# Moving w2 and the two halves of h by 128 bytes in the expert stage's on-chip memory layout

## The chip, the cores and the metric

The kernel runs on one core of a Trainium2 chip. The metric is the device time of one execution in microseconds (us). TensorE (PE in the rows) does the matrix products, VectorE (DVE) and ScalarE (ACT) the elementwise work, GpSimd (POOL) issues scattered transfers, SyncE (SP) the other ones.

## The reference

```
X = rfft(x, axis=1)                       # x: 8 x 2496 x 256
Yr = Xr @ w_r - Xi @ w_i + b_r            # and Yi likewise; soft threshold 0.01 on both
t = irfft(Yr + i*Yi).reshape(19968, 256)  # the tokens
expert = argmax(t @ w_gate); g = its softmax weight
out[token] = g * (relu(token @ w1[expert]) @ w2[expert])   # 8 experts, 256 -> 1024 -> 256
```

All inputs are float32. The first four lines are the spectral stage, the last one is the expert stage.

## The kernel before, in words

The spectral stage transforms batch after batch and scatters each token's row into a list of its expert in DRAM. The expert stage then works through tiles of 256 tokens of one expert each; 82 tiles run. Every float32 operand of a product is split into a high part, rounded to the format in which TensorE takes one column per step, and a low part, the rest. Products are sums of three partial products.

A tile of the expert stage gives TensorE three streams, always in this order:

- the **up stream**, line 1097: 48 matmuls of 256 columns. The moving operand is the tile's input, `xh` or `xl`; the stationary operand, loaded by a weight load (LDWEIGHTS) before each matmul, is 128 columns of w1, `h1` or `l1`. The order is (h1, xh), (l1, xh), (h1, xl), for two halves of the depth and eight groups of 128 hidden units.
- the **wide stream**, line 1137: 16 matmuls of 512 columns. Moving is `h2`, in which w2's high and low part lie side by side; stationary is the high half of h, `hh`.
- the **low stream**, line 1139: 16 matmuls of 256 columns. Moving is the high part of w2 in `h2`; stationary is the low half of h, `hl`.

ScalarE makes `hh` from the up stream's sums (line 1102), VectorE makes `hl` (line 1103). From the eighth tile on the wide and low streams run for both halves of the tile's tokens together: 16 wide matmuls in a row, then 16 low ones. The tiles before it, whose work is interleaved with the end of the spectral stage, and the last tile go through `down`'s loop over `h`: 8 wide, 8 low, and the same again.

All of these tiles lie in the pool `w2p`. The function `skip` allocates a small unused tile, so that what comes after it starts at a chosen byte offset. The sums of the allocations give these offsets, modulo 256 bytes:

| tile | used as | before | after |
|---|---|---|---|
| `h1`, `l1` (pool `k2`) | stationary, up | 0 | 0 |
| `xh`, `xl` | moving, up | 192 | 192 |
| `h2` (w2) | moving, wide and low | 64 | 192 |
| `hh` | stationary, wide | 64 | 192 |
| `hl` | stationary, low | 128 | 0 |
| `xf`, the transposed input | not read by TensorE | 64 | 192 |
| `o`, `part` | not read by TensorE | 128 | 0 |

Every slice that a matmul or a weight load takes of these tiles starts a multiple of 512 bytes behind the tile, so the offset of a tile is that of all its slices. In the spectral stage line 413 multiplies with moving w at offset 192 and stationary `sh` or `sl` at 0, and line 345 has both operands at 192.

Of the kernel before, what the change touches and what calls it, by code (L numbers as in the profile page):

```python
# [99 lines left out]
class Kernel:  # L100
# [849 lines left out]
    def open_experts(self, st):  # L950
        self.w2p = self.pool(st, "w2p", 1, side="right")
        self.psa = self.pool(st, "psa", 2, side="right", space=PSUM)
        self.psb = None
        self.wide = False
        self.r2 = [self.w2p.tile([128, 4, D], F32, name=f"r2{q}") for q in range(2)]
        self.weights(0, 2)
        self.skip(self.w2p, 64)
        self.h2 = self.w2p.tile([128, 8, 2, D], F32R, name="h2")

    def word(self, j, t, top):  # L960
# [94 lines left out]
    def upright(self, t):  # L1055
        if t >= self.nt:
            return
        nc = self.nc
        xf = self.w2p.tile([128, 2, 8, 32], F32, tag="xf", name="xf")
        nc.vector.transpose(xf.rearrange("p c t j -> p t c j"), self.xqs.pop(t))  # L1060
        yield
        xf = xf.rearrange("p c t j -> p c (t j)")
        if not t:
            self.skip(self.w2p, 128)
        xh = self.w2p.tile([128, 2, TT], F32R, tag="xh2", name="xh2", bufs=2)
        xl = self.w2p.tile([128, 2, TT], F32R, tag="xl2", name="xl2", bufs=2)
        with self.tc.high_priority():
            nc.scalar.copy(xh, xf)
        yield
        with self.tc.high_priority():  # L1070
            nc.vector.tensor_sub(xl, xf, xh)
        self.xts[t] = (xh, xl)

    def up(self, t, work=()):
        work = iter(work)
        nc = self.nc
        xh, xl = self.xts.pop(t)
        h1, l1 = self.h1, self.l1
        if t and self.psb:
            self.split2(t)  # L1080
        if not t:
            self.skip(self.w2p, 192)
        hh = self.w2p.tile([128, 8, TT], F32R, tag="hh", name="hh")
        if not t:
            self.skip(self.w2p, 64)
        hl = self.w2p.tile([128, 8, TT], F32R, tag="hl", name="hl")
        for f2 in range(4):
            if f2 % 2 and self.wide:
                p = self.psi.tile([128, 512], F32, tag="u", name="ph", bufs=4).rearrange("p (i t) -> p i t", i=2)
            else:  # L1090
                p = (self.psb if self.psb and f2 % 2 else self.psa).tile([128, 2, TT], F32, tag="h", name="ph")
            for i in range(2):
                f = f2 * 2 + i
                m = 0
                for c in range(2):
                    for a, v in ((h1, xh), (l1, xh), (h1, xl)):
                        nc.tensor.matmul(p[:, i, :], a[:, c, f * 128:(f + 1) * 128], v[:, c, :],  # L1097
                                         start=m == 0, stop=m == 5)
                        m += 1
            s = slice(f2 * 2, f2 * 2 + 2)  # L1100
            with self.tc.high_priority():
                nc.scalar.activation(hh[:, s, :], p, AF.Relu)  # L1102
                nc.vector.scalar_tensor_tensor(out=hl[:, s, :], in0=p, scalar=0.0, in1=hh[:, s, :],  # L1103
                                               op0=ALU.max, op1=ALU.subtract)
            next(work, None)
            if t and f2 % 2 == 0 and not self.psb:
                self.split2(t, (f2, f2 + 1))
            if t > 1 and f2 % 2:
                self.pace(hh.bitcast(F32)[0:1, f2 * 2, 0:1])
                self.send(1)  # L1110
            yield
        self.hs[t] = (hh, hl)

    def down(self, t):
        tc, nc = self.tc, self.nc
        hh, hl = self.hs.pop(t)
        w2 = self.h2
        xr = self.xrs.pop(t)
        if t >= self.early:
            row = self.w2p.tile([128, 2], I32, tag="row", name="row", bufs=2)  # L1120
            nc.vector.tensor_tensor(out=row, in0=xr.bitcast(I32)[:, :, 1], in1=self.drop[:, t - self.early, :],
                                    op=ALU.add)
            at = [row[:, h:h + 1] for h in range(2)]
        else:
            at = [xr.bitcast(I32)[:, h, 1:2] for h in range(2)]
        o = self.w2p.tile([128, 2, D], F32, tag="o", name="o", bufs=2)
        if t == self.early:
            self.skip(self.w2p, 32)

        def bank():  # L1130
            return (self.psb.tile([128, 512], F32, tag="o", name="po") if self.psb else
                    self.psi.tile([128, 512], F32, tag="u", name="po", bufs=4))

        def product(p, h, f, wide):
            hs = slice(h * 128, (h + 1) * 128)
            if wide:
                nc.tensor.matmul(p, hh[:, f, hs], w2[:, f].rearrange("p a d -> p (a d)"), start=f == 0, stop=False)  # L1137
            else:
                nc.tensor.matmul(p[:, :D], hl[:, f, hs], w2[:, f, 0, :], start=False, stop=f == 7)  # L1139

        def give(p, h):
            part = self.w2p.tile([128, D], F32, tag="part", name="part", bufs=2)
            nc.scalar.activation(part, p[:, D:], AF.Copy, scale=xr[:, h, 0:1])  # L1143
            nc.vector.scalar_tensor_tensor(out=o[:, h, :], in0=p[:, :D], scalar=xr[:, h, 0:1], in1=part,  # L1144
                                           op0=ALU.mult, op1=ALU.add)
            i = nc.gpsimd.indirect_dma_start(  # L1146
                out=self.out[:, :], out_offset=bass.IndirectOffsetOnAxis(ap=at[h], axis=0),
                in_=o[:, h, :], in_offset=None, bounds_check=self.ntok - 1, oob_is_err=False)
            if t or h:
                tc.declare_no_dep(i.ins, group="out", reason="every token is in one tile only")  # L1150
            tc.add_to_no_dep_group("out", i.ins)

        if self.psb and t < self.final:
            ps = [bank() for _ in range(2)]
            for wide in (True, False):
                for f in range(8):
                    for h in range(2):
                        product(ps[h], h, f, wide)
                if wide:
                    self.split1(t + 1)  # L1160
                    yield
            for h in range(2):
                give(ps[h], h)
            yield
            return
        for h in range(2):
            p = bank()
            for wide in (True, False):
                for f in range(8):
                    product(p, h, f, wide)  # L1170
                if wide and t < 2:
                    yield
            if not h:
                self.split1(t + 1)
            give(p, h)
            yield
# [56 lines left out]
```

## Time and profile before

| | us |
|---|---|
| median of 3 runs (1460.29 to 1462.82) | 1460.95 |
| the profiled execution | 1460.41 |
| its span, first to last instruction | 1458.6 |
| TensorE busy in it | 1436.8 |
| VectorE, ScalarE, GpSimd busy | 926.7, 767.5, 477.9 |

Matmuls are pipelined: a matmul's duration in a row (277 ns for one of line 1097) reaches into the next one. What a stream costs is read from the starts of its matmuls: the time from the first start of one stream to the first start of the next, divided by the count.

### The profile page before, as it was taken

How to read it: one execution, taken by the hardware profiler on the slowest of the kernel's cores; microseconds unless marked ns; L12 is line 12 of the kernel's file. 1: busy time of each engine (PE TensorE's matmuls, PEld its weight loads, DVE VectorE, ACT ScalarE, POOL GpSimd, SP SyncE). 2: the span in 40 equal slices, each digit the busy share in tenths (PEclk: the TensorE clock that was granted, in tenths of full speed). 3: DMA queues.
4: the chain of work that ended last, by engine and by line, in shares of the span. 5: the costliest groups of instructions: out<-in, count | busy, mean ns of one | idle time of the engine just before them, and what ended most of it. 6: DMA issues, size and time to landing. Idle time of an engine off the chain costs nothing. (4 is left out here: it accounts for less than half of the span.)

```text
span 1458.6 us, 34965 instructions
## 1 busy us (share of the span) xinstructions
PE 1436.8 (99%) x10551; PEld 1310.5 (90%) x10552; DVE 926.7 (64%) x1951; ACT 767.5 (53%) x1537; POOL 477.9 (33%) x594
## 2 busy tenths in 40 slices
PE   8999999999999999999999999999999999999997
PEld 4889898898989878899999999999999999999996
DVE  3788898988998876554565645454545445445443
ACT  2778787787877764444443434343434334334332
POOL 3042466656574354343311211211211121111111
PEclk9999999999999999999999999999999999999999
DMA  7974465556555333344332423233223223232210
GB/s 230 251 229 129 138 188 161 162 168 174 159 157 152 73 100 100 96 126 126 96 107 74 111 50 100 77 81 98 58 49 97 50 55 99 51 82 68 50 48 21
DMA packets 194337, 161.99 MB, mean 111 GB/s; under 512 B 128011, under 2 KB 164531, under 8 KB 194128
## 3 DMA queue, kind: packets, MB, share of 16 engines
q1 hardware_dynamic: 173616, 113.37, 30.7%
q0 software_dynamic: 20512, 46.20, 9.3%
q8 instruction: 87, 1.43, 0.4%
q14 instruction: 122, 1.00, 0.2%
HBM read 241.99 MB, written 66.37 MB: 211 GB/s over the span
## 5 line engine op out<-in xcount | busy, mean ns | idle before, releaser
L1097 PE MATMUL ph<-xh,h 128*128 128x256 f32 x1312 | 363.6, 277 | 0.0
L1097 PE MATMUL ph<-xl,h 128*128 128x256 f32 x1312 | 363.2, 277 | 0.0
L1097 PE MATMUL ph<-xh,l 128*128 128x256 f32 x1312 | 363.1, 277 | 0.0
L1137 PE MATMUL po<-h,hh 128*128 128x512 f32 x1312 | 313.5, 390 | 0.4 <-DVE h L1036 0.4
L1146 POOL DMA_INDIRECT out<-o,row x124 | 121.7, 981 | 558.0 <-DVE o L1144 527.4
L1103 DVE SCALAR_TENSOR_TENSOR hl<-ph,hh 128x512 fp32r<-128x512 f32 x328 | 225.9, 689 | 110.5 <-ACT hh L1102 95.8
L1137 PEld LDWEIGHTS po<-h,hh 128*128 128x128 f32 x1312 | 239.4, 188 | 46.9 <-ACT hh L1102 1.5
L1102 ACT ACTIVATE hh<-ph 128x512 fp32r<-128x512 f32 x328 | 193.9, 598 | 160.7 <-PE ph L1097 113.0
L1144 DVE SCALAR_TENSOR_TENSOR o<-po,xr,part 128x256 f32<-128x256 f32 x156 | 68.7, 480 | 311.6 <-ACT part L1143 309.3
L1097 PEld LDWEIGHTS ph<-xh,h 128*128 128x128 f32 x1312 | 247.0, 188 | 0.5 <-issue 0.3
L1143 ACT ACTIVATE part<-po,xr 128x256 f32<-128x256 f32 x156 | 66.0, 471 | 344.5 <-PE po L1139 312.6
L1097 PEld LDWEIGHTS ph<-xh,l 128*128 128x128 f32 x1312 | 246.3, 188 | 0.2
L1097 PEld LDWEIGHTS ph<-xl,h 128*128 128x128 f32 x1312 | 246.3, 188 | 0.0
L831 POOL DMA_INDIRECT xs_dram<-yb,pos x176 | 177.8, 1010 | 58.5 <-issue 46.9
L1139 PEld LDWEIGHTS po<-h,hl 128*128 128x128 f32 x1312 | 167.0, 189 | 6.9
L1139 PE MATMUL po<-h,hl 128*128 128x256 f32 x1312 | 169.3, 281 | 0.0
L447 DVE SCALAR_TENSOR_TENSOR y<-v,r 64x256 f32<-64x256 f32 x320 | 133.6, 417 | 5.7 <-ACT r L441 0.6
L467 ACT COPY z<-pv 128x256 f32<-128x256 f32 x160 | 93.9, 708 | 0.1
L770 POOL COPY mark<-y 1x1 f32<-1x1 f32 x72 | 25.3, 351 | 203.9 <-DVE y L447 203.9
L463 PE MATMUL pv<-bi,y 128*128 128x128 f32 x640 | 86.6, 277 | 2.6 <-DVE y L447 2.5
L380 PEld LDWEIGHTS pb<-bm,t 128*128 128x128 f32 x640 | 78.2, 191 | 11.1 <-DVE mx L787 3.4
L380 PE MATMUL pb<-bm,t 128*128 128x128 f32 x640 | 86.7, 278 | 1.3 <-DMA t<-spec_dram 1.3
(204 smaller groups left out, 2465.7 us busy)
## 6 DMA issues: line engine op xcount, KB each, us to landing
r<-moe_w SPq DMA_DIRECT2D x672, 128.0 KB
r<-moe_w SPq DMA_DIRECT2D x166, 512.0 KB
xq<-xs_dram SPq DMA_DIRECT2D x332, 64.0 KB
t<-spec_dram SPq DMA_DIRECT2D x160, 128.0 KB
spec_dram<-ae SPq DMA_DIRECT2D x77, 240.0 KB
x<-x SPq DMA_DIRECT2D x38, 384.0 KB
x<-x SPq DMA_DIRECT2D x38, 84.0 KB
xs_dram<-yb,pos POOLq DMA_INDIRECT x176, 2.9
```

The costliest lines, as they stand in the source:

```text
L380: nc.tensor.matmul(p[:, c, :, kp, :], t[:, kp, c * 128:(c + 1) * 128], self.bm[:, 2 * s + kp, :], start=True, stop=True)
L447: nc.vector.scalar_tensor_tensor(out=y[q * 64:q * 64 + 64, kp, :], in0=u[h, q, :], scalar=LAM, in1=r[h, q, :], op0=ALU.add, op1=ALU.min)
L463: nc.tensor.matmul(p[:, c, kp, :, :], y[:, kp, c * 128:(c + 1) * 128], self.bi[:, 2 * s + kp, :], start=True, stop=True)
L467: nc.scalar.copy(self.zs[b % 2][:, c, 0:NB, 4 * s:4 * s + 4].rearrange("p n a -> p a n"), p[:, c].rearrange("p a r n -> p (a r) n"))
L831: i = nc.gpsimd.indirect_dma_start(out=self.xs[:, :], out_offset=bass.IndirectOffsetOnAxis(ap=pos[:n, g:g + 1], axis=0), in_=y[:n, g, :], ...
L1097: nc.tensor.matmul(p[:, i, :], a[:, c, f * 128:(f + 1) * 128], v[:, c, :], start=m == 0, stop=m == 5)
L1102: nc.scalar.activation(hh[:, s, :], p, AF.Relu)
L1103: nc.vector.scalar_tensor_tensor(out=hl[:, s, :], in0=p, scalar=0.0, in1=hh[:, s, :], op0=ALU.max, op1=ALU.subtract)
L1137: nc.tensor.matmul(p, hh[:, f, hs], w2[:, f].rearrange("p a d -> p (a d)"), start=f == 0, stop=False)
L1139: nc.tensor.matmul(p[:, :D], hl[:, f, hs], w2[:, f, 0, :], start=False, stop=f == 7)
L1144: nc.vector.scalar_tensor_tensor(out=o[:, h, :], in0=p[:, :D], scalar=xr[:, h, 0:1], in1=part, op0=ALU.mult, op1=ALU.add)
L1146: i = nc.gpsimd.indirect_dma_start(out=self.out[:, :], out_offset=bass.IndirectOffsetOnAxis(ap=at[h], axis=0), in_=o[:, h, :], in_offset=N ...
```

## The change

Four calls of `skip` change, one of them goes away. No tile changes its size, the pool keeps its total (480 bytes are skipped before and after), and no instruction is added, removed or moved on any engine: the rows of both programs differ in line numbers and buffer numbers alone, so there is no piece of the order to show. What changes is the byte offset that the table above lists: `h2` moves up by 128 bytes, `hh`, `hl`, `o` and `part` move down by 128.

```
@@ open_experts
         self.weights(0, 2)
-        self.skip(self.w2p, 64)
+        self.skip(self.w2p, 192)
         self.h2 = self.w2p.tile([128, 8, 2, D], F32R, name="h2")
@@ upright
         xf = xf.rearrange("p c t j -> p c (t j)")
-        if not t:
-            self.skip(self.w2p, 128)
         xh = self.w2p.tile([128, 2, TT], F32R, tag="xh2", name="xh2", bufs=2)
@@ up
         if not t:
-            self.skip(self.w2p, 192)
+            self.skip(self.w2p, 64)
         hh = self.w2p.tile([128, 8, TT], F32R, tag="hh", name="hh")
         if not t:
             self.skip(self.w2p, 64)
         hl = self.w2p.tile([128, 8, TT], F32R, tag="hl", name="hl")
@@ down
         if t == self.early:
-            self.skip(self.w2p, 32)
+            self.skip(self.w2p, 160)
```

## Rows read from the trace of the kernel before

**Rows 1.** The page: busy time by engine, and TensorE's granted clock in 40 slices.

```profile
span 1458.6 us, 34965 instructions
PE 1436.8 (99%) x10551; PEld 1310.5 (90%) x10552; DVE 926.7 (64%) x1951; ACT 767.5 (53%) x1537; POOL 477.9 (33%) x594
PEclk9999999999999999999999999999999999999999
```

**Rows 2.** Busy time by engine in a stretch of the expert stage.

```profile
core 0: us, PE busy (x) PEld busy (x) DVE busy (x) ACT busy (x) POOL busy (x), PEclk, DMA share, GB/s
640.00:1440.00 800.00, 800.00 (x5829) 754.54 (x5828) 409.22 (x732) 323.25 (x599) 160.26 (x175) 1.00 0.30 77
```

**Rows 3.** Groups of TensorE's instructions, 640 to 1440 us.

```profile
line engine op names shapes xcount | busy us, mean ns | idle before us <-releasers
L1097 PE MATMUL ph<-xl,h 128*128 128x256 f32 x1165 | 322.1, 276 | 0.0
L1137 PE MATMUL po<-h,hh 128*128 128x512 f32 x1168 | 276.5, 389 | 0.0
L1139 PE MATMUL po<-h,hl 128*128 128x256 f32 x1168 | 149.7, 281 | 0.0
```

**Rows 4.** TensorE in order of time, one tile's end and the next up stream.

```profile
start us, us, engine line op out<-in xcount [idle before <-releaser]
1004.28 3.79 PE L1137 MATMUL po<-h,hh 128*128 128x512 f32 x16
1007.90 2.05 PE L1139 MATMUL po<-h,hl 128*128 128x256 f32 x16
1009.79 0.28 PE L1097 MATMUL ph<-xh,h 128*128 128x256 f32 x1
...
1010.49 0.28 PE L1097 MATMUL ph<-xh,h 128*128 128x256 f32 x1
...
1015.26 3.79 PE L1137 MATMUL po<-h,hh 128*128 128x512 f32 x16
1018.88 2.05 PE L1139 MATMUL po<-h,hl 128*128 128x256 f32 x16
```

**Rows 5.** VectorE and ScalarE in order of time: the last `hl` and `hh` before these.

```profile
1005.11 0.69 DVE L1103 SCALAR_TENSOR_TENSOR hl<-ph,hh 128x512 fp32r<-128x512 f32 x1
1004.48 0.60 ACT L1102 ACTIVATE hh<-ph 128x512 fp32r<-128x512 f32 x1 [0.76 <-PE ph L1097]
```

**Rows 6.** TensorE in order of time: first and last up stream behind 16 low matmuls.

```profile
636.47 0.28 PE L1097 MATMUL ph<-xh,h 128*128 128x256 f32 x1
...
1438.01 0.28 PE L1097 MATMUL ph<-xh,h 128*128 128x256 f32 x1
```

**Rows 7.** TensorE in order of time: two up streams of earlier tiles, with their neighbours.

```profile
613.06 1.10 PE L1139 MATMUL po<-h,hl 128*128 128x256 f32 x8
614.01 0.28 PE L1097 MATMUL ph<-xh,h 128*128 128x256 f32 x1
...
619.66 2.08 PE L1137 MATMUL po<-h,hh 128*128 128x512 f32 x8
...
625.27 0.28 PE L1097 MATMUL ph<-xh,h 128*128 128x256 f32 x1
...
630.92 3.83 PE L1137 MATMUL po<-h,hh 128*128 128x512 f32 x16
634.58 2.05 PE L1139 MATMUL po<-h,hl 128*128 128x256 f32 x16
```

**Rows 8.** TensorE in order of time: wide and low streams of one earlier tile.

```profile
574.21 1.07 PE L1139 MATMUL po<-h,hl 128*128 128x256 f32 x8
575.11 2.00 PE L1137 MATMUL po<-h,hh 128*128 128x512 f32 x8
576.95 1.10 PE L1139 MATMUL po<-h,hl 128*128 128x256 f32 x8
577.89 0.28 PE L1097 MATMUL ph<-xh,h 128*128 128x256 f32 x1
```

**Rows 9.** TensorE in order of time, spectral stage: lines 413, 345 and 500.

```profile
185.15 0.28 PE L413 MATMUL pk<-wlr,sh 128*128 128x256 f32 x1
...
185.74 0.39 PE L345 MATMUL pa<-xah,feh 78*120 78x512 f32 x1
...
186.44 0.40 PE L500 MATMUL py<-zh,gh 120*117 120x512 f32 x1
...
369.87 0.28 PE L413 MATMUL pm<-wld,sh 128*128 128x256 f32 x1
...
371.12 0.39 PE L500 MATMUL py<-zh,gh 120*117 120x512 f32 x1
```

More of the change, by code (lines that the diff above doesn't have):

```diff
@@ L956, in open_experts @@
         self.weights(0, 2)
-        self.skip(self.w2p, 64)
+        self.skip(self.w2p, 192)
         self.h2 = self.w2p.tile([128, 8, 2, D], F32R, name="h2")
@@ L1062, in upright @@
         xf = xf.rearrange("p c t j -> p c (t j)")
-        if not t:
-            self.skip(self.w2p, 128)
         xh = self.w2p.tile([128, 2, TT], F32R, tag="xh2", name="xh2", bufs=2)
@@ L1081, in up @@
         if not t:
-            self.skip(self.w2p, 192)
+            self.skip(self.w2p, 64)
         hh = self.w2p.tile([128, 8, TT], F32R, tag="hh", name="hh")
@@ L1127, in down @@
         if t == self.early:
-            self.skip(self.w2p, 32)
+            self.skip(self.w2p, 160)
         def bank():
```

## Prediction

> **What bounds the kernel now.** I read the page first: TensorE is busy for 99% of the span, with the granted clock at nine tenths or more in every slice [rows 1]. The table by stretches says it more sharply of the expert stage: from 640 to 1440 us TensorE is busy for all 800 us at a granted clock of 1.00, the upper of its two levels (2.4 GHz), VectorE for 409 and ScalarE for 323 [rows 2], and the groups of that stretch show no idle time before any of the three streams [rows 3]. So nothing there waits for data. The time is the number of matmuls times the pace at which TensorE starts them, and the pace is what a change of addresses can touch.
>
> The rows in order of time give the paces. In the tile of [rows 4] the wide stream's 16 matmuls take 1007.90 - 1004.28 = 3.62 us, 226 ns each. The 16 low ones take 1009.79 - 1007.90 = 1.89 us, 118 ns each. The up stream that follows takes 1015.26 - 1009.79 = 5.47 us for 48; its first six take 0.70 us (117 ns each), the other 42 take 4.77 us (113.6 ns each). The next low stream starts 10.98 us after this one. From the first of these up streams to the last are 801.54 us [rows 6], which is 73 times 10.98: there are 74, all of the same length. Whatever the change does to one tile is paid or gained 74 times.
>
> So matmuls of 256 columns have two paces: a **fast** one near 113.5 ns and a **slow** one near 117.8 ns. The same line shows both with the same tiles: two up streams of earlier tiles take 5.65 us for 48 (614.01 to 619.66 and 625.27 to 630.92), 117.7 ns from end to end [rows 7]. So does the low stream: 8 in 0.90 us at 574.21, 112.5 ns, and 8 in 0.94 us at 576.95, 117.5 ns [rows 8]. Nothing else that the rows show differs between these streams. I read this as a pattern of the two reads that run side by side, the moving operand and the weight load for the next matmul: once a stream has fallen into the slow pattern it repeats it, and it leaves it only if something breaks the repetition.
>
> **The change part by part.** No instruction is added or removed, so there are no costs to add up but those of pace.
>
> *Inside the low stream.* Before, the moving operand is at 64 and the weight load at 128, 64 bytes further. After, 192 and 0: again 64 further, modulo 256. Up reads at 192 and 0 too. Both pairs show both paces, and the same two: 112.5 and 118 for the pair 64/128 [rows 4, 8], 113.6 and 117.7 for 192/0 [rows 4, 7]. Line 413, also 192/0, repeats it in the spectral stage: 5 in 0.59 us from 185.15, 118 ns, and 11 in 1.25 us from 369.87, 113.6 ns [rows 9]. So the distance of the two reads counts and not the place, and the low stream should be no faster than now. It enters from the same neighbour, a wide stream with equal offsets, as it does now; all its entries from a settled wide stream in these rows are slow. Term: 0. Bounds: if it turned fast, -16 x 4.4 ns = -0.07 us a tile; nothing in the rows makes it slower than its 118 ns.
>
> *Inside the wide stream.* Both offsets are equal before (64/64) and after (192/192). Term 0, with a small addition at its start, below.
>
> *The seam from low to up.* This is where I see the change. Before, the last low matmul reads w2 at 64, the weight load beside it reads h1 at 0, 64 bytes behind it instead of ahead, and the next moving operand jumps from 64 to 192. After, the last low matmul reads at 192, the weight load at 0 is 64 ahead, and the next moving operand is at 192: the seam looks exactly like any step inside the low stream and inside the up stream. Now the slow pattern ends six matmuls behind the seam [rows 4], so the seam is the likely thing that breaks it. After the change nothing breaks it, and the up stream carries the low stream's slow pace through all 48, as the two of [rows 7] do. Cost: 5.65 - 5.47 = 0.18 us a tile by those rows. Each start is rounded to 0.01; by paces it is 42 x (117.7 - 113.6) = 0.17, and with 113.1, half of what the wide stream takes for 512 columns, 0.19. I take 0.185. Times 74: **+13.7 us**; the bounds 0.17 and 0.20 give 12.6 and 14.8.
>
> *The seam from up to wide.* Before, the up stream reads at 192 beside a weight load at 64; after, both are at 192. A slow up stream ahead of a wide one costs the wide one something today: 3.66 us instead of 3.62 behind the slow up stream [rows 4, 7]. With 192/192 the nearest row is line 345 behind a slow line 413: three of 512 columns in 0.70 us, 233 ns each, against 226, with narrower tiles [rows 9]. So 0 to 0.04 us a tile, 0 to 3.0 us in all. I take 0: those are other tiles, and the 0.02 us that the three lose is as much as the rounding of two starts.
>
> *The other tiles.* `xf`, `o`, `part` are touched by VectorE and ScalarE, which are busy half the time. The last `hl` is ready at 1005.80 and the first low matmul starts at 1007.90; the last `hh` is ready at 1005.08, 2.8 us before the wide stream ends [rows 4, 5]. A slower write of some tens of ns would stay under that. Term 0. The two slow up streams of [rows 7] belong to tiles that use the loop over `h`, of which there are eight; there is little left to lose in them, and I leave them out.
>
> *The sum* is made against the profiled execution, 1460.41 us (span 1458.6, the other 1.8 around it): 1460.4 + 13.7 = 1474.1. The median of the runs shown is 0.5 higher, so I expect **1474.6 us**.
>
> **A rule against it.** The rows show two paces for one shape with the same operands [rows 3, 4, 7]. The Trainium skill, TensorE: Matmul & The Clock Gate, section Step-by-step: what each phase is for, says that TensorE has two independent read ports, so that loading the next weights takes no read bandwidth from the running matmul. By that rule no offset could matter, and the sum would stay at 1460.95. The Trainium skill, same page, section Back-to-back issue gap, has one gap for 256 columns, by its formula an estimate of 109 ns; the trace has two, both above it.
>
> **The rivals.**
>
> *No change.* The slow pattern may be broken at the seam by something else than the offsets: the jump to another bank of the sums, or the wait at the head of the up stream. For it: in the earlier tiles the offsets at the seam are the same, and the up stream stays slow [rows 7, 8]; only behind 16 low matmuls in a row does it let go. So the seam's offsets are not enough, the step of the pattern at which the seam falls counts too. Against it: the earlier tiles have a wait and a change of bank there as well. Or the offsets have no part in the pace at all; against that stands that one line with the same tiles has two paces. Either way 1461 us.
>
> *Faster: the low stream turns fast.* If the place of the two reads counts and not only their distance (h2 and `hl` change their distance by 256 bytes), the low stream may settle behind the wide one. It gains 16 x 4.4 = 0.07 us, and the first six of the up stream another 0.02: 0.09 x 74 = 6.7 us, so 1454.3. It decides if the first two or three low matmuls come at 113 ns. For it: the low stream can run at 112.5 [rows 8]. Against: after a settled wide stream it does not, in all the tiles with 16.
>
> *Slower by less.* The wide stream may not settle: 8 take 1.84 us in an earlier tile [rows 8], so 16 would lose about 0.06 us, 4.4 us in all, 1465.3; or the slow pattern breaks part of the way through the up stream.
>
> **How the numbers follow.** Slow up streams 0.78, with 1472 to 1479 as their own range (0.17 to 0.20 a tile, and up to 3 us for the wide stream's start). No change 0.09 (0.07 for another cause at the seam, 0.02 for offsets without any part). Low stream fast 0.07. Slower by less 0.06. To leave no more than 2 in 10 out, the range takes in the last case: 1464 to 1480. A measurement of this kernel tells about 0.2%, 2.9 us, from no change. Faster by more 0.08, within it 0.09, slower by more 0.83.
>
> **What would show it.** Right: up streams behind 16 low matmuls take 5.65 us, mean duration 281 ns as the low ones now instead of 276, a tile takes 11.16 us, low and wide keep 1.89 and 3.62, and everything up to some 530 us is as before. Wrong: up streams of 5.47 us, or low streams of 1.82.

## The result, and the profile after

The changed kernel takes 1477.76 us (median of 5 runs, 1476.83 to 1477.91). The kernel before, beside it on the same chip, takes 1460.95 (1460.29 to 1463.09). The ratio is 1.011, with a 95% interval of 1.0099 to 1.0121: slower by 16.8 us. The forecast was 1474.6 us with a range of 1464 to 1480.

The page of the profiled execution (1477.47 us) shows the same work in a longer span; TensorE is busy for 16.1 us more than in [rows 1], with the same granted clock in every slice:

```profile
span 1475.6 us, 34966 instructions
PE 1452.9 (98%) x10552; PEld 1324.5 (90%) x10552; DVE 926.7 (63%) x1951; ACT 765.4 (52%) x1537; POOL 479.0 (32%) x594
PEclk9999999999999999999999999999999999999999
```

The groups of TensorE's instructions from 640 to 1440 us, beside [rows 3]. Up, wide and low are lines 1095, 1135 and 1137 here:

```profile
line engine op names shapes xcount | busy us, mean ns | idle before us <-releasers
L1095 PE MATMUL ph<-xl,h 128*128 128x256 f32 x1146 | 322.2, 281 | 0.0
L1135 PE MATMUL po<-h,hh 128*128 128x512 f32 x1145 | 273.1, 391 | 0.0
L1137 PE MATMUL po<-h,hl 128*128 128x256 f32 x1136 | 145.4, 281 | 0.0
```

The up matmuls have the low ones' mean, 281 ns in place of 276, the wide ones 391 in place of 389, the low ones are as they were, and still nothing stands in front of them. In order of time, one tile:

```profile
start us, us, engine line op out<-in xcount [idle before <-releaser]
643.32 3.82 PE L1135 MATMUL po<-h,hh 128*128 128x512 f32 x16
646.97 2.05 PE L1137 MATMUL po<-h,hl 128*128 128x256 f32 x16
648.85 0.28 PE L1095 MATMUL ph<-xh,h 128*128 128x256 f32 x1
...
654.51 3.81 PE L1135 MATMUL po<-h,hh 128*128 128x512 f32 x16
```

Wide takes 646.97 - 643.32 = 3.65 us (3.62 in [rows 4]), low 648.85 - 646.97 = 1.88 (1.89), up 654.51 - 648.85 = 5.66 (5.47). That is 11.19 us a tile in place of 10.98, and nearly all of the difference stands in the up stream. For the sum, the first up stream of all (the spectral stage runs until then), the first behind 16 low matmuls, and the last:

```profile
531.76 0.39 PE L1095 MATMUL ph<-xh,h 128*128 128x256 f32 x1
...
637.66 0.28 PE L1095 MATMUL ph<-xh,h 128*128 128x256 f32 x1
...
1454.77 0.28 PE L1095 MATMUL ph<-xh,h 128*128 128x256 f32 x1
```

and the first up stream of the kernel before:

```profile
530.65 0.39 PE L1097 MATMUL ph<-xh,h 128*128 128x256 f32 x1
```

From 637.66 to 1454.77 are 817.11 us, 73 tiles of 11.193; in [rows 6] they are 801.54, 73 of 10.980. So the span's 17.0 us (1475.6 - 1458.6) come like this: 15.6 from 73 tiles at 0.213; 0.2 behind the last up stream's start, itself a slow one (20.8 us to the end of the span, 20.6 before); 1.1 ahead of 531.76, most of which is there after 100 us (TensorE is busy for 92.19 us of them, for 93.02 before), long before the expert stage begins; and 0.1 between there and 637.66.

### The profile page after: what moved, and what is told of

It is laid out like the page before. It is cut to its first block, busy times and chain, and to the rows that moved or that the text cites. A ratio compares the mean times of both kernels' runs of the same rounds, so it can differ in the third digit from the quotient of the medians.

```text
span 1475.6 us, 34966 instructions
## 1 busy us (share of the span) xinstructions
PE 1452.9 (98%) x10552; PEld 1324.5 (90%) x10552; DVE 926.7 (63%) x1951; ACT 765.4 (52%) x1537; POOL 479.0 (32%) x594
## 5 line engine op out<-in xcount | busy, mean ns | idle before, releaser
L1095 PE MATMUL ph<-xh,h 128*128 128x256 f32 x1312 | 368.9, 281 | 0.0
L1095 PE MATMUL ph<-xl,h 128*128 128x256 f32 x1312 | 368.7, 281 | 0.0
L1095 PE MATMUL ph<-xh,l 128*128 128x256 f32 x1312 | 368.6, 281 | 0.0
L1095 PEld LDWEIGHTS ph<-xh,h 128*128 128x128 f32 x1312 | 251.4, 192 | 0.5 <-issue 0.3
```

## The experiments

Theory: an up stream carries on at the pace of the low stream in front of it, unless the seam between them breaks the pattern; the change takes away what broke it. Rivals: the new places as such are slow, or something else at the seam ends the slow pattern. The kernel before took 1470.9 us beside runs 1 to 4, 1461.9 beside 5 to 8, 1471.1 beside 9 and 10, 1470.3 beside 11 and 1461.6 beside 12, so each ratio is to the executions taken together with the run. The tiles are no part of that difference: run 2 has the tile of [rows 4], and 9.4 of the 11.7 us by which its span is longer stand between its first up stream (532.67) and its first one behind 16 low matmuls (647.91). All times of streams below are differences of starts in the view of TensorE in order of time, near 1000 us. A **jump** is a change of the moving operand's offset from one stream to the next. Edits are shown against the kernel before, that of run 12 against run 11; `...` stands for lines left out, and from run 6 on the last `skip`, which keeps the rest of the pool in its place, is left out too.

### 1. The up pair follows, and the places stay

`h1`, `l1` go from 0 to 128, `xh2`, `xl2` from 192 to 64; the last two calls keep the rest where it was.

```
-        self.skip(k2, 544)
+        self.skip(k2, 416)
...
-        if not t:
-            self.skip(self.w2p, 128)
...
-            self.skip(self.w2p, 192)
+            self.skip(self.w2p, 64)
...
-            self.skip(self.w2p, 32)
+            self.skip(self.w2p, 288)
```

> The kernel before with the up stream's pair moved instead: xh2/xl2 at 64 and h1/l1 at 128, w2 and hh left at 64 and hl at 128. Nothing stands at 192 or 0 any more, but the seam from low to up now looks like a step inside either stream. Theory of the seam: up streams behind 16 low matmuls stay slow, 5.65 us for 48 (mean duration 281 ns), a tile takes 11.16 to 11.20 us, the time is 1474 to 1479 us. Rival, the place: what slows is w2 at 192 with hl at 0, which this kernel does not have; then up streams take 5.47 us and the time is 1461 us.

1485.62 us, ratio 1.0103 (1.0086 to 1.012). Its rows:

```profile
1001.61 0.28 PE L1095 MATMUL ph<-xh,h 128*128 128x256 f32 x1
...
1007.27 3.81 PE L1135 MATMUL po<-h,hh 128*128 128x512 f32 x16
1010.92 2.05 PE L1137 MATMUL po<-h,hl 128*128 128x256 f32 x16
1012.80 0.28 PE L1095 MATMUL ph<-xh,h 128*128 128x256 f32 x1
```

Up takes 5.66 us, wide 3.65, low 1.88: the changed kernel's times, with nothing but up's own operands (and the buffers beside `h1`) moved. `o` and `part` are where they were before, so they have no part in it. The place of w2 and `hl` is out.

### 2. The seam of before, at the places of after

`h2` and `hh` stand at 192 and `hl` at 0, as in the change; `xh2`, `xl2` at 64, `h1`, `l1` at 128.

```
-        self.skip(k2, 544)
+        self.skip(k2, 416)
...
-        self.skip(self.w2p, 64)
+        self.skip(self.w2p, 192)
...
-            self.skip(self.w2p, 32)
+            self.skip(self.w2p, 160)
```

> The kernel after, with the up stream's pair moved too: w2 and hh at 192, hl at 0 as in the change, xh2/xl2 at 64 and h1/l1 at 128. At the seam the last weight load is again 64 behind the moving operand, and the moving operand jumps by 128, as in the kernel before. Theory of the seam: the up streams let go after some six matmuls, 5.47 us for 48, a tile of 10.98 us, 1461 us. Rival, the place of w2 and hl: it stays at 1477 us, with up streams of 5.65 us.

1470.84 us, ratio 0.9998 (0.9988 to 1.0008), in spite of w2 and `hh` at 192 and `hl` at 0. Its rows:

```profile
1004.93 3.79 PE L1137 MATMUL po<-h,hh 128*128 128x512 f32 x16
1008.56 2.05 PE L1139 MATMUL po<-h,hl 128*128 128x256 f32 x16
1010.45 0.28 PE L1097 MATMUL ph<-xh,h 128*128 128x256 f32 x1
...
1015.91 3.79 PE L1137 MATMUL po<-h,hh 128*128 128x512 f32 x16
```

Wide 3.63, low 1.89, up 5.46: the times of [rows 4], with every offset turned by half of 256. With run 1 this settles the change: what counts is how the offsets of neighbouring streams stand to each other, not where they are, as far as a turn by 128 bytes can tell.

### 3. The high half alone

`h2` and `hh` go to 192, `hl` stays at 128, up's pair at 192 and 0.

```
-        self.skip(self.w2p, 64)
+        self.skip(self.w2p, 192)
...
-        if not t:
-            self.skip(self.w2p, 128)
...
-            self.skip(self.w2p, 192)
+            self.skip(self.w2p, 64)
...
-            self.skip(self.w2p, 64)
+            self.skip(self.w2p, 192)
```

> One part of the change alone: w2 and hh go to 192, hl stays at 128. The moving operand is then at 192 on both sides of the seam (no jump), but the weight load goes from 64 behind to 64 ahead there. Theory that the jump of the moving operand breaks the slow pattern: up streams slow, 5.65 us, 1475 to 1479 us if the low stream keeps 1.89 us. Rival, that the change of the weight load's distance breaks it: up streams of 5.47 us, 1461 us. Open by both: the low stream reads its weights 64 behind, which no row has shown; 1.82 us (fast) to 1.89 us, which would take up to 5 us off either time.

1483.31 us, ratio 1.0089 (1.0072 to 1.0106). Up 5.65 us, wide 3.66, low 1.88. There is no jump, and the up stream stays slow, although the weight load goes from 64 behind to 64 ahead at the seam. The low stream reads its weights 64 behind its moving operand here and keeps its pace: at 64 bytes the sign of the distance makes no difference to it.

### 4. Eight low matmuls in a row, the offsets of before

```
-        if self.psb and t < self.final:
+        if False:
```

> The kernel before, all its offsets as they are, with the down products in the order of the earlier tiles in every tile: 8 wide and 8 low for one half, then for the other. The last low matmul then falls at another step of the slow pattern. Theory that the seam breaks the pattern only at one step of it: up streams slow as in the earlier tiles, +0.185 us a tile, the first 8 low fast (0.90 us in place of 0.94, -0.04 us), the second wide stream up to 0.03 us longer: a tile of 11.1 to 11.2 us, 1470 to 1477 us. Rival, that the offsets at the seam are enough: up streams of 5.47 us, 1457 to 1461 us.

1489.43 us, ratio 1.0126 (1.0109 to 1.0143). Its rows:

```profile
1005.45 0.28 PE L1097 MATMUL ph<-xh,h 128*128 128x256 f32 x1
...
1011.10 2.01 PE L1137 MATMUL po<-h,hh 128*128 128x512 f32 x8
1012.95 1.11 PE L1139 MATMUL po<-h,hl 128*128 128x256 f32 x8
1013.90 2.00 PE L1137 MATMUL po<-h,hh 128*128 128x512 f32 x8
1015.73 1.10 PE L1139 MATMUL po<-h,hl 128*128 128x256 f32 x8
```

The seam has the jump of before, 64 to 192, and up still takes 5.65 us. So the jump is not enough; the matmul at which it falls counts, as the earlier tiles of [rows 7] had it. The miss is in the low streams: the first eight aren't fast (0.95 us, not 0.90), and both wide streams of a tile (1.85 and 1.83 us for 8) pay for a start, so the tile has 11.23 us and is slower than the changed kernel's.

### 5. The jump, with no weight load falling behind

`h1` and `l1` go to 128.

```
-        self.skip(k2, 544)
+        self.skip(k2, 416)
```

> The kernel before with h1/l1 alone moved, from 0 to 128. At the seam from low to up the moving operand still jumps from 64 to 192, but the weight load beside the last low matmul is 64 ahead of it, as inside the low stream; inside the up stream the weights are now 64 behind. Theory that the jump of the moving operand is enough (at the step at which 16 low matmuls end): up streams of 5.47 us, tile of 10.98 us, the same time as before. Rival, that the jump and a weight load that falls behind are needed together: up streams slow, 5.65 us, a tile of 11.16 to 11.20 us, 1.009 to 1.011 of before.

1478.93 us, ratio 1.0112 (1.0095 to 1.0129). Its rows:

```profile
1006.27 2.05 PE L1139 MATMUL po<-h,hl 128*128 128x256 f32 x16
1008.15 0.28 PE L1097 MATMUL ph<-xh,h 128*128 128x256 f32 x1
...
1013.81 3.83 PE L1137 MATMUL po<-h,hh 128*128 128x512 f32 x16
```

Up 5.66 us, low 1.88, wide 3.67. The jump falls behind the 16th low matmul as before, and up stays slow: the offset of up's weights counts too. Whether it counts at the seam is not shown, since up's weights also stand 64 behind all through the up stream here, not 64 ahead.

### 6 and 7. Other distances for the low stream's weights

The skip ahead of `hl`, which puts it at 128, is left out in run 6 (`hl` at 64, as w2), and doubled in run 7 (`hl` at 192):

```
-            self.skip(self.w2p, 64)
+            self.skip(self.w2p, 128)
```

> The kernel before with hl alone moved from 128 to 64: the low stream's weights at the same offset as its moving operand. Theory that the weights' distance has no part inside a stream, as the run with the high half alone has it: the low stream stays slow with 1.89 us, up 5.47 us, a tile of 10.98 us, 1.000 of before. Rival, that a distance of 0 lets the low stream run fast, as the wide one does with 0: low 1.81 to 1.83 us, a tile of 10.89 to 10.93 us if up is fast throughout, 0.994 to 0.997 of before.

1462.99 us, ratio 1.0004 (0.9994 to 1.0013). Its rows:

```profile
1006.89 3.79 PE L1135 MATMUL po<-h,hh 128*128 128x512 f32 x16
1010.52 2.08 PE L1137 MATMUL po<-h,hl 128*128 128x256 f32 x16
1012.43 0.28 PE L1095 MATMUL ph<-xh,h 128*128 128x256 f32 x1
...
1017.88 3.79 PE L1135 MATMUL po<-h,hh 128*128 128x512 f32 x16
```

Low takes 1.91 us, 0.02 more than before, and up 5.45, 0.02 less: it lets go at once. Both theories had something wrong: a distance of 0 is not the same as 64, but it is no better.

> The kernel before with hl alone moved from 128 to 192, half of 256 bytes away from the moving operand. Theory that the weights' distance has no part inside a stream: low 1.89 us, up 5.47 us, a tile of 10.98 us, 1.000 of before. Rival, that this distance matters: low of 1.82 us or less if it frees the reads (0.994 to 0.997 of before), or another, slower pace; the up stream then enters at another step and may stay slow, 1.008 to 1.011 of before.

1479.4 us, ratio 1.0115 (1.0098 to 1.0132). Its rows:

```profile
1003.11 3.80 PE L1137 MATMUL po<-h,hh 128*128 128x512 f32 x16
1006.74 2.09 PE L1139 MATMUL po<-h,hl 128*128 128x256 f32 x16
1008.67 0.28 PE L1097 MATMUL ph<-xh,h 128*128 128x256 f32 x1
...
1014.32 3.79 PE L1137 MATMUL po<-h,hh 128*128 128x512 f32 x16
```

Low takes 1.93 us, the slowest of all runs, and the up stream, of whose operands nothing was moved, 5.65 us in place of 5.47: what it inherits has changed.

### 8. The jump inside the low stream

`h2a` stands at 64, `h2b` at 192; `hh` is cut in the same way into 64 and 192, `hl` into 128 and 0.

```
-        self.h2 = self.w2p.tile([128, 8, 2, D], F32R, name="h2")
+        h2a = self.w2p.tile([128, 2, 2, D], F32R, name="h2a")
+        self.skip(self.w2p, 128)
+        h2b = self.w2p.tile([128, 6, 2, D], F32R, name="h2b")
```

> The jump put where it should help more: w2, hh and hl each in two tiles, w2 and hh at 64 for the first quarter of f and at 192 for the rest, hl at 128 and then at 0. The low stream then makes the jump of 128 behind its 4th matmul, which by a pattern of three steps is the same step as the 16th; the rest of it reads as the kernel after does, and the seam from low to up has no jump. Theory that the jump at that step breaks the slow pattern: low matmuls from the 11th on at 113 ns, the low stream 1.86 us, the up stream fast from its first matmul, 5.44 us; the wide stream has a jump behind its 4th matmul too, which costs 0 to 0.03 us: a tile of 10.92 to 10.96 us, 0.996 to 0.999 of before. Rival, that a slow low stream needs the change of operands at the seam, from hl and w2 to h1 and xh2, to be broken: low 1.89 us, up 5.65 us, a tile of 11.16 to 11.22 us, 1.009 to 1.013 of before.

1476.16 us, ratio 1.0093 (1.0076 to 1.011). Low 1.88 us, its last twelve 1.41 (117.5 ns each), up 5.66, wide 3.63. The jump did not break the pattern here. A second jump that I hadn't counted, from w2 at 192 at the wide stream's end to 64, lies in front of the first low matmul, so the fourth need not be at the step that I took it for.

### 9 and 10. Distances of 32

The skip ahead of `hl` is 32 in run 9 (`hl` at 96), and 224 in run 10 (`hl` at 32):

```
-            self.skip(self.w2p, 64)
+            self.skip(self.w2p, 32)
```

> The kernel before with hl alone at 96: the low stream's weights 32 bytes ahead of its moving operand, between the 0 and the 64 that were run. Theory that the distance sets the low stream's slow pace, and that a stream that enters behind a settled wide one falls into it at any distance: 117.8 to 120 ns a matmul, low 1.89 to 1.92 us; up lets go at once or after six, 5.45 to 5.47 us, or not at all, 5.65; a tile of 10.98 to 10.99 us, 1.000 to 1.001 of before, or 11.17 to 11.19, 1.009. Rival, that there is a distance at which the low stream settles as the wide one does: 113.3 ns, low 1.81 us, up 5.44 to 5.47 us, a tile of 10.88 to 10.91 us, 0.993 to 0.995 of before.

1486.25 us, ratio 1.0108 (1.0091 to 1.0125). Low 1.89 us, up 5.65, wide 3.63.

> The kernel before with hl alone at 32: the low stream's weights 32 bytes behind its moving operand. The same two theories. The pace is set by the distance and always slow: low 1.89 to 1.92 us, a tile of 10.98 to 10.99 us (1.000 to 1.001 of before) if the up stream lets go, 11.17 to 11.19 (1.009) if it doesn't. Rival, a distance at which the low stream settles: low 1.81 us, a tile of 10.88 to 10.91 us, 0.993 to 0.995 of before.

1486.15 us, ratio 1.01 (1.0083 to 1.0117). Low 1.87 us, a little faster than with 32 ahead (so at 32 bytes the sign does count), up 5.65, wide 3.67. No distance that was run makes the low stream settle behind the wide one, and behind the jump none but 0 and the 64 of before lets the up stream go.

### 11. Low begins as in run 6, and jumps into what up is there

`h2b` (`f` 6 and 7) stands at 64, `h2a` (`f` 0 to 5) at 192; `hh` is cut in the same way into 64 and 192, `hl` into 64 and 0.

```
-        self.h2 = self.w2p.tile([128, 8, 2, D], F32R, name="h2")
+        h2b = self.w2p.tile([128, 2, 2, D], F32R, name="h2b")
+        self.skip(self.w2p, 128)
+        h2a = self.w2p.tile([128, 6, 2, D], F32R, name="h2a")
...
-                for f in range(8):
+                for f in range(8) if wide else (6, 7, 0, 1, 2, 3, 4, 5):
```

> The seam at which the up stream let go at once, put into the low stream: w2, hh and hl each in two tiles, the last quarter of f with w2, hh and hl at 64 (no distance), the rest with w2 and hh at 192 and hl at 0, and the low products begin with the last quarter. The first four low matmuls then run as in the run with hl at no distance, the next twelve and the up stream read as that up stream does, with no jump between them. Theory that the jump out of that pattern lets the next stream settle, whichever it is: first four low about 118 to 120 ns, the others 113.3, low 1.83 to 1.85 us; up fast from the first, 5.44 us; wide 0.01 us longer for a jump behind its 12th matmul: a tile of 10.91 to 10.93 us, 0.996 to 0.997 of before. Rival, that it needs the first group of sums of the up stream or its other operands: low 1.89 us, up 5.47 us or slow with 5.65, a tile of 10.99 to 11.20 us, 1.001 to 1.011 of before.

1468.67 us, ratio 0.9983 (0.997 to 0.9997): the fastest of all. Its rows:

```profile
1006.32 2.92 PE L1143 MATMUL po<-h2a,hha 128*128 128x512 f32 x12
1009.07 1.07 PE L1143 MATMUL po<-h2b,hhb 128*128 128x512 f32 x4
1009.98 0.64 PE L1145 MATMUL po<-h2b,hlb 128*128 128x256 f32 x4
1010.45 1.53 PE L1145 MATMUL po<-h2a,hla 128*128 128x256 f32 x12
1011.82 0.28 PE L1104 MATMUL ph<-xh,h 128*128 128x256 f32 x1
...
1017.25 2.92 PE L1143 MATMUL po<-h2a,hha 128*128 128x512 f32 x12
```

The four low matmuls at no distance take 0.47 us, the twelve behind the jump 1.37 (114.2 ns each, in place of 118), and the up stream, with no jump in front of it, 5.43 us: it carries on at a fast pace as it carries on at a slow one in the changed kernel. The wide stream gives part of it back, 3.66 us in place of 3.62, where 0.01 was expected; there is no jump in front of it either. A tile takes 10.93 us, 0.05 less than before by these rows; 10.94 as the mean of two (1022.75 - 1000.88 = 21.87 us from up stream to up stream), and 74 times 0.04 us are 3.0 us, the 0.2% that the runs show, which their interval only just tells from nothing. The profiled execution shows less than that: it is the second slowest of the eleven (1471.84 us), its 73 tiles from 648.34 to 1449.41 take 10.97 us on the average, and the wide stream waits for ScalarE's `hh` three times in it, 1.2 us in all, where TensorE waited for nothing in the kernel before.

### 12. The same, with the jump ahead of up and of wide

Against run 11: `h1`, `l1` go to 128, `xh2`, `xl2` to 64, and the skip ahead of `hh` keeps the rest.

```
-        self.skip(k2, 544)
+        self.skip(k2, 416)
...
+        if not t:
+            self.skip(self.w2p, 128)
...
-            self.skip(self.w2p, 64)
+            self.skip(self.w2p, 192)
```

> The kernel of the run before (low starts at no distance) with the up stream's pair moved: xh2/xl2 at 64, h1/l1 at 128. The up stream then ends with a jump into the wide one, as in the kernel before, where the wide stream starts without loss (without that jump it loses 0.03 us); the price is that the fast low stream now ends with a jump into up. Theory that a jump hurts only as it does between a fast up stream and the wide one (4 ns): up stays fast, 5.44 to 5.45 us, wide 3.64 us, a tile of 10.91 to 10.93 us, 0.995 to 0.998 of before. Rival, that a jump out of a fast stream into one of 256 columns drops it into the slow pattern: up 5.65 us, a tile of 11.12 to 11.14 us, 1.006 to 1.010 of before.

1475.11 us, ratio 1.0092 (1.0078 to 1.0106): the rival. Its rows:

```profile
1004.43 1.53 PE L1147 MATMUL po<-h2a,hla 128*128 128x256 f32 x12
1005.80 0.28 PE L1106 MATMUL ph<-xh,h 128*128 128x256 f32 x1
...
1011.45 2.93 PE L1145 MATMUL po<-h2a,hha 128*128 128x512 f32 x12
```

The last twelve low matmuls are as fast as in run 11 (1.37 us), then comes the jump, and the up stream takes 5.65 us. A jump can break the fast pattern as well as the slow one. (The wide stream did not gain: 1003.96 - 1000.29 = 3.67 us.)

### All of them together

```
kernel     jump low->up   low us   up us   wide us   ratio
before     yes            1.89     5.47    3.62      1
after      no             1.88     5.66    3.65      1.011
run 1      no             1.88     5.66    3.65      1.0103
run 2      yes            1.89     5.46    3.63      0.9998
run 3      no             1.88     5.65    3.66      1.0089
run 4      yes, 8 low     0.95     5.65    1.85      1.0126
run 5      yes            1.88     5.66    3.67      1.0112
run 6      yes            1.91     5.45    3.63      1.0004
run 7      yes            1.93     5.65    3.63      1.0115
run 8      no             1.88     5.66    3.63      1.0093
run 9      yes            1.89     5.65    3.63      1.0108
run 10     yes            1.87     5.65    3.67      1.01
run 11     no             1.84     5.43    3.66      0.9983
run 12     yes            1.84     5.65    3.67      1.0092
```

Without a jump the up stream has the pace in which the low one ends, five times out of five: slow behind slow (after, runs 1, 3 and 8), fast behind fast (run 11, the only kernel for this half). With a jump it is fast three times (before, runs 2 and 6) and slow six times (runs 4, 5, 7, 9, 10 and 12).

A rival that no run addresses is that reads and writes of the other engines set the paces. The traces, whose starts are whole ns, speak against it: from 640 to 1440 us all 73 up streams of the kernel before take 5465 or 5466 ns, and all 71 of the changed kernel 5655 or 5656, although VectorE's load differs along the way (53.72 us busy from 800 to 900 us in the kernel before, 49.50 from 1000 to 1100).

## Why the prediction was right, by its own steps

**The seam from low to up** carried the forecast: take away the jump, and the up stream keeps the low stream's pace through all 48. The runs show it against the rival of no change: without the jump slow at the old places (run 1), with it fast at the new ones (run 2), and neither a bank nor a wait was touched. The term was 0.185 us a tile; up measures 5.66 against 5.47, 0.19, with 0.01 taken back by low. The doubt that the text kept, that the step of the pattern at the seam counts too, was in place: run 4. Only half of the step holds beyond this case. Without a jump nothing broke the slow pattern in four kernels of four, but a jump behind a slow low stream broke it in only three of eight; that the kernel before had one that did is owed to its particular offsets, and the forecast needed only that it goes away.

**Inside the low stream** the term of 0 was right (1.88 against 1.89). Its reason, that the distance of the two reads counts and not the place, holds as far as it was needed, since the change keeps 64 ahead, and run 2 turns all places without effect. But the distance tells less than the text made of it: -64 and 64 give one pace (run 3), 0 and 128 two others (runs 6 and 7), and 32 and -32 differ from each other (runs 9 and 10).

**The seam from up to wide** is the term that was mis-sized. Taken as 0 with 0.04 as its bound, it measures 3.65 against 3.62, 0.03 us, 2.2 us in 74 tiles. The row that pointed to it, line 345 behind line 413 with 0.02 us lost in three matmuls, was set aside as rounding. The slow up stream alone does not decide it, as the text's comparison with [rows 4, 7] had it. Where the moving operand goes on unchanged from up to wide, wide takes 3.65 or 3.66 every time, behind slow up streams (after, runs 1 and 3) as behind the fast one (run 11). Where it jumps, wide takes 3.62 or 3.63 behind a fast up stream (before, runs 2 and 6), and behind a slow one 3.63 three times (runs 7, 8 and 9) and 3.67 three times (runs 5, 10 and 12).

**The other tiles**: 0 was right, since run 1 has `o` and `part` as before and is slow, and run 2 has them as after and is not.

What remains of the 17.0 us beside 73 or 74 tiles is the 1.1 us ahead of the first up stream. It need not belong to the change: in the profiled executions of all fourteen kernels, none of which changes the spectral stage, the first up stream starts anywhere from 530.65 to 534.42 us. The forecast fell 3.2 us short, nearly all of it for these two, the wide stream's start and the 1.1 us; the terms of up and low were right to 0.01 us a tile.

What stays open is why a pattern lasts, and which step of it a jump has to meet. The starts in ns show that there are patterns, and more than one: the settled low stream's steps are 120, 123 and 117 ns over and over in many tiles of run 7, 120 ns each time in run 6, and three of them make 360 ns in both, where three fast steps of the kernel before make 340. Nor was it tried whether offsets repeat with 256 bytes, as the tables have it; that the low stream kept 1.88 us when `h2` and `hl` moved apart by 256 agrees with it. The runs show that the pace of a stream depends on the offsets of both reads in it and on the stream before it; no view shows the reads themselves.

## What to carry to other kernels

When TensorE is the bound and nothing waits, divide a stream's length by its matmuls before anything else: two paces for one shape are time that no schedule shows. Compare the offsets of neighbouring streams, not only those of one instruction: in these kernels a stream of 256 columns kept the pace of the one of 256 columns before it where the moving operand's offset went on unchanged, and nothing here foretells what a change of it does, so try the few offsets and read the pace of each stream, which a single profile tells to 0.01 us. A layout that looks more even can be the slower one.

## What the runs showed of the hardware

The address of the weights alone changes the pace of the matmuls beside them. Runs 6 and 7 move `hl` and nothing else that TensorE reads, and the 16 low matmuls take 1.91 and 1.93 us in place of 1.89. The Trainium skill, TensorE: Matmul & The Clock Gate, section Step-by-step: what each phase is for, says that loading the next weights takes no read bandwidth from the running matmul; these runs disagree, as far as that is to mean that the matmuls keep one pace wherever the weights lie.

A matmul of 256 columns ran at 113.1 ns in the best stream (5.43 us for 48 in run 11) and at 120.6 in the worst (1.93 us for 16 in run 7), at a granted clock of 1.00 in both. The up stream took 5.43 us in run 11 and 5.66 in the changed kernel with the same tiles at the same offsets: the pace of all its 48 matmuls depended on the stream before it.
